# Queueing the second feed-forward's weight transfers on GpSimd instead of SyncE

## The chip, the cores and the metric

The kernel runs on one core of a Trainium2 chip. Five engines work side by side, each through its own instruction queue in order: TensorE (PE, matrix products), VectorE (DVE), ScalarE (ACT), GpSimd (POOL) and SyncE (SP, which only starts transfers). A transfer (DMA) is started by an instruction in the queue of SP, POOL or ACT and is then carried out by the core's 16 DMA engines. An instruction that has to wait holds up everything behind it in its own queue. The metric is the device time of one execution in microseconds (us); lower is better.

## The reference

Three stages follow each other; batch 4, 8 heads, 768 positions, 40 features per head.

```python
# 1: recurrence over the positions, one 40x40 state per batch and head
for t in range(S):
    y[:, :, t] = einsum('bhd,bhde->bhe', rt, state)
    Sa = einsum('bhde,bhe->bhd', state, at)
    state = state * wt[:, :, None, :] - einsum('bhd,bhe->bhde', Sa, bt)
    state = state + einsum('bhd,bhe->bhde', vt, kt)
x = y.transpose(0, 2, 1, 3).reshape(3072, 320)
# 2: first feed-forward (w1, w2: 320x1024, w3: 1024x1024, w_out: 1024x320)
x = ((x @ w1) * (x @ w2)) @ w3 @ w_out
# 3: second feed-forward (w_in: 320x2048, w_out: 2048x320)
h = maximum(x @ w_in, 0.0)
out = (h * h) @ w_out
```

The feed-forward weights arrive as 64-bit floats, so they take twice the bytes of the arithmetic.

## The kernel before

The recurrence is worked in 24 chunks of 32 positions. Chunk c runs through the stages `do_x0`, `do_sa`, `do_sat`, `do_l`, `do_z` and `do_ys`, which are chained by matrix products on PE and by copies on ACT and DVE. Between the stages PE is filled with other work from a queue of items: for every two chunks the first feed-forward of 256 tokens (`a_tile`, "ab" products at line 382 and "px" products at line 440). So PE's order in this first phase is a written one, and a product that waits holds up both kinds of work. The first phase takes about the first 696 us. In the second phase, PE runs the second feed-forward alone (`b_h` and `b_o`, "ph" and "po").

Three side streams feed the first phase.

- Preparation of later chunks (`prep`, `prep_pq`, `prep_kb`), six chunks ahead. From chunk 10 on its transfers are queued on POOL: the image of a chunk is loaded (`im<-img`, line 553), multiplied on POOL (lines 595 and 601), and then PE multiplies it in `prep_pq` (line 614). The results go to scratch tensors in DRAM.
- Loads and stores of each chunk on SP: `KB_d` and `Q_d` (scratch), `YR`, `YI`, `wt`, `XL`, `RX`, `vs` and `RT` for the next chunk, then the store of the chunk's output, `X_d<-yst` (line 837, two halves). After every second chunk `a_tile` loads two chunks' output back (`xf<-X_d`, `xr<-X_d`, lines 393 and 395), and PE's next "ab" product waits for it through a copy on ACT (`xh`, line 369).
- Weights. `fetch` loads a piece of a 64-bit weight into a staging buffer `raw` (line 326). ACT takes its two words apart (lines 334 and 335), DVE joins them to a 32-bit float (lines 339 and 342), and ACT and POOL split it into a high and a low part (`wuh`/`wul` at lines 966 and 967, `wih`/`wil` at 352 and 353, `wir` at 365 and 366).

The variable `early` is true while the weights of the first feed-forward are fetched. It is set to False at line 978, before the 36 fetches of the second feed-forward: 16 of `wo2` (320 KB each; the trace cuts digits off and names it `wo`), 4 of the last 64 rows of `win` (two transfers of 128 KB each) and 16 of `win` (256 KB each), 40 transfers in all. They share 5 `raw` buffers and 4 `wst` buffers, so fetch n+5 cannot load before line 342 of fetch n is through.

The kernel's scheduler sets the order in each queue. In the kernel before, the first five of these transfers stand on SP at chunk 3, where the memory of the first feed-forward's staging comes free (after the last `w2r` split, line 366 on POOL). The other 35 stand on SP between the loads and stores of chunks 18 to 23 and of the second phase's first input (`b_load`, line 954).

Of the kernel before, what the change touches and what calls it, by code (L numbers as in the profile page):

```python
# [245 lines left out]
def body(tc, img, rv, rd, vn, vp, raw, w1, w2, w3t, wo, win, wo2, ident, maskt, out, dbg=None):  # L246
    nc = tc.nc
    mm = nc.tensor.matmul
    act, dve, pool, sp = nc.scalar, nc.vector, nc.gpsimd, nc.sync

    with (
# [12 lines left out]
        with right, tc.manual_schedule(engines={mybir.EngineType.PE}):  # L264
# [8 lines left out]
            def staged(pl, tags, words):  # L273

                slots, n = staging.setdefault(tags, (deque(), [0]))
                if not slots:
                    t = pl.tile([128, 2048], U32, name="early", tag=tags[n[0] % len(tags)])
                    n[0] += 1
                    slots.extend(t[:, i:i + words] for i in range(0, 2049 - words, words))
                return slots.popleft()  # L280

            staging = {}
            early = True
# [14 lines left out]
            def fetch(pl, K, N, parts, dst=None, tag="fold"):  # L298

                place = None  # L300
                if early:
                    count[tag] += 1
                    if tag == "split" and count[tag] <= SPLIT_STAGED:
                        place = staged(ma, ("gh", "gl"), 1024)
                    elif tag == "fold" and not w12 and count[tag] <= FOLD_STAGED:
                        place = staged(wa, ("w1h", "w1l", "w2h"), 640)
                signed = early
                tag = "split" if early and tag == "split" else "wst"
                if dst is not None:
                    o = dst  # L310
                else:
                    o = pl.tile([128, K, N], F32, name="wst", tag=tag, bufs=bufs[tag])
                if not is64:
                    for p, f, src in parts:
                        sp.dma_start(out=o[p, f], in_=src)
                    return o
                if place is not None:
                    rt = place[:, 0:2 * K * N]
                else:
                    rt = pl.tile([128, 2 * K * N], U32, name="raw", tag="raw", bufs=bufs["raw"])  # L320
                rv_ = rt.rearrange("p (k n) -> p k n", k=K)
                at_ = MID + count["late"] // EACH
                count["late"] += not early
                with behind(mids.get(at_ - 2)):
                    for p, f, src in parts:
                        sp.dma_start(out=rv_[p, f], in_=src)
                w2_ = rt.rearrange("p (k n j) -> p k n j", k=K, j=2)
                hi, lo = w2_[:, :, :, 1], w2_[:, :, :, 0]
                top = rt.bitcast(F16).rearrange("p (k n j) -> p k n j", k=K, j=4)[:, :, :, 1]
                ou = o.bitcast(U32)  # L330


                with tc.issue_after(gate[-1]) if early and gate else behind(mids.get(min(at_, NCH - 1))), tc.issue_after(gate[-2]) if early and len(gate) > 2 else nullcontext():
                    act.activation(out=o, in_=hi.bitcast(F32), func=AF.Copy, scale=2.0 ** -112)
                    act.activation(out=lo, in_=lo, func=AF.Copy, scale=2.0 ** -29, bias=LOW)  # L335
                    if signed:
                        act.activation(out=top, in_=hi.bitcast(F32), func=AF.Copy, scale=2.0 ** -60)
                with tc.issue_after(hold[-1]) if hold else nullcontext():
                    dve.scalar_tensor_tensor(out=ou, in0=ou, scalar=3, in1=lo, op0=ALU.logical_shift_left,  # L339
                                             op1=ALU.bitwise_or)  # L340
                    if not signed:
                        dve.scalar_tensor_tensor(out=ou, in0=hi, scalar=0x80000000, in1=ou, op0=ALU.bitwise_and,
                                                 op1=ALU.bitwise_or)
                return o

            def split_w(pl, src, h, l, j, k):

                n = 512 if early else 256

                t = fetch(pl, 1, n, [(slice(0, 128), 0, wcols(src, n * j, n)[128 * k:128 * k + 128])], tag="split")  # L350
                f = slice(n * j, n * j + n)
                act.copy(out=h[:, k, f], in_=t[:, 0])
                pool.tensor_tensor(out=l[:, k, f], in0=t[:, 0], in1=h[:, k, f], op=ALU.subtract)

            def split_r(pl, two):

                n = 512 if early else 256


                t = fetch(pl, 1, n, [(slice(64 * i, 64 * i + 64), 0, wcols(src, c, n)[256:320])  # L360
                                       for i, (src, c, _) in enumerate(two)], tag="split")
                for i, (_, c, r) in enumerate(two):
                    p, q = slice(64 * i, 64 * i + 64), slice(64 - 64 * i, 128 - 64 * i)
                    f = slice(c, c + n)
                    act.copy(out=r[p, f], in_=t[p, 0])
                    pool.tensor_tensor(out=r[q, f], in0=t[p, 0], in1=r[p, f], op=ALU.subtract)
# [90 lines left out]
            def fold(solved):  # L457
# [5 lines left out]
                def load_w3(i):  # L463
                    f, g = i // 2, i % 2
                    w3[i] = fetch(wf, 4, 128, [(slice(0, 128), slice(0, 4), wcols(w3t, 128 * f, 128)[
                        512 * g:512 * g + 512, :].rearrange("(k p) f -> p k f", p=128))])
# [40 lines left out]
            with (  # L507
# [394 lines left out]
                for c in range(NCH):  # L902
                    last = c == NCH - 1
                    p = c + 6
# [73 lines left out]
            early = False  # L978
# [190 lines left out]
```

## Time and profile before

| What | Value |
|---|---|
| median of 3 runs | 1052.82 us (1050.34 to 1056.4) |
| profiled execution, its own time | 1051.49 us |
| span of the profile, first to last instruction | 1049.6 us |
| mean granted TensorE clock | 0.964 |
| PE busy | 912.6 us, 87% |
| DVE busy | 684.0 us, 65% |
| ACT busy | 476.3 us, 45% |
| POOL busy | 222.2 us, 21% |
| chain that ended last | PE 54%, DVE 19%, DMA 11%, ACT 9%, issue 4%, SP's queue 1%, POOL 1% |

All times in the rows are counted from the start of the span. The busy share of PE is an average over two different phases: in the last 350 us PE hardly pauses, while in the first phase it pauses a few us at a time, where a chunk's chain, a load or a split arrives late. A queue named SPq is SP's, POOL's own instructions appear as POOL or POOLq. In a row of the timeline the number in brackets is the time for which the engine stood still before the instruction, and what released it.

### The profile page before, as it was taken

What the parts mean: (1) busy time and instruction counts of PE and PEld (TensorE: products, weight loads), DVE (VectorE), ACT (ScalarE), POOL (GpSimd) and SP (SyncE); (2) the same over time, 40 slices, a digit from 0 to 9 for tenths busy, and PEclk for the clock granted to TensorE, in tenths of its full rate; (3) what the DMA queues carried; (4) which work ended last, traced back from release to release, by engine and by line L of the source; (5) the groups of instructions that cost most, each with busy time, mean ns of one, the idle gap of its engine ahead of it and who ended that gap; (6) DMA issues with size and microseconds to landing.
All of it is one profiled execution on the core that took longest, in us unless ns stands there. A gap on an engine that the chain in (4) does not pass through costs nothing.

```text
span 1049.6 us, 29232 instructions
## 1 busy us (share of the span) xinstructions
PE 912.6 (87%) x12240; PEld 818.8 (78%) x12240; DVE 684.0 (65%) x1366; ACT 476.3 (45%) x975; POOL 222.2 (21%) x304
## 2 busy tenths in 40 slices
PE   1346676898899899899999889999999999999996
PEld 1235454688899788789988879889899999999996
DVE  8753689569869977996798655753555554444432
ACT  2845776343353334435355546643433333434332
POOL 0242125443444343443202112310000000000000
PEclk9999688899999999989999989899999999999999
DMA  8988875665667567766665753631223121000001
GB/s 225 304 241 214 222 214 157 186 173 150 148 185 183 148 156 196 182 152 171 149 146 151 196 125 100 175 76 36 31 62 69 58 36 26 1 26 1 25 2 27
DMA packets 209389, 134.44 MB, mean 128 GB/s; under 512 B 143793, under 2 KB 184114, under 8 KB 209252
## 3 DMA queue, kind: packets, MB, share of 16 engines
q1 hardware_dynamic: 201892, 110.61, 41.3%
q0 software_dynamic: 7072, 21.57, 7.1%
q8 instruction: 98, 1.61, 0.7%
q10 hardware_dynamic: 288, 0.33, 0.1%
q14 instruction: 39, 0.32, 0.1%
HBM read 99.27 MB, written 33.19 MB: 126 GB/s over the span
## 4 chain that ended last, share of the span: by engine, by line
PE 54%; DVE 19%; DMA 11%; ACT 9%; issue 4%; SPq 1%; POOL 1%; ACTq 0%; DVEq 0%; POOLq 0%
PE ph L382 17%; PE po L1029 16%; PE ab L382 9%; PE px L440 4%; DMA im<-img 4%; DVE T L678 2%; DVE tmp L675 2%; DVE yst L834 2%; DMA raw<-w3t 2%; DVE RX L830 2%; PE pat L822 2%; PE pat L793 1%; ACT raw L335 1%; DVE wst L339 1%; DMA early<-w 1%
## 5 line engine op out<-in xcount | busy, mean ns | idle before, releaser
L1029 PE MATMUL po<-wul,rh 128*128 128x320 f32 x384 | 118.1, 308 | 0.0
L1029 PE MATMUL po<-wuh,rh 128*128 128x320 f32 x384 | 118.0, 308 | 0.0
L1029 PE MATMUL po<-wuh,rl 128*128 128x320 f32 x384 | 117.3, 307 | 0.0
L382 PE MATMUL ph<-xh,wih 128*128 128x512 f32 x192 | 75.7, 394 | 0.7 <-issue 0.7
L382 PE MATMUL ph<-xh,wil 128*128 128x512 f32 x192 | 75.3, 392 | 0.0
L382 PE MATMUL ph<-xl,wih 128*128 128x512 f32 x192 | 74.9, 390 | 0.0
L1029 PEld LDWEIGHTS po<-wul,rh 128*128 128x128 f32 x384 | 72.0, 188 | 3.6
L1029 PEld LDWEIGHTS po<-wuh,rh 128*128 128x128 f32 x384 | 72.0, 188 | 3.5
L419 ACT CAST gh<-g 128x256 fp32r<-128x256 f32 x96 | 38.9, 405 | 75.8 <-DVE g L414 69.5
L1029 PEld LDWEIGHTS po<-wuh,rl 128*128 128x128 f32 x384 | 71.8, 188 | 0.0
L440 PE MATMUL px<-wph,gh 128*128 128x320 f32 x192 | 66.5, 346 | 5.5 <-DVE x L445 4.6
L678 DVE TENSOR_TENSOR T<-T,tmp 128x31 f32<-128x31 f32 (+20 forms) x170 | 66.4, 391 | 3.5
L675 DVE TENSOR_TENSOR tmp<-PT,T 128x31 f32<-128x31 f32 (+20 forms) x170 | 64.2, 378 | 3.7
L420 DVE TENSOR_TENSOR gl<-g,gh 128x256 fp32r<-128x256 f32 x96 | 47.5, 497 | 26.6 <-ACT gh L419 26.1
L413 ACT COPY a_sb<-ab 128x256 f32<-128x256 f32 x96 | 35.6, 371 | 63.4 <-PE ab L382 62.9
L382 PE MATMUL ab<-xh,w1h 128*128 128x256 f32 x192 | 58.9, 307 | 6.0 <-ACT xh L369 5.9
L822 PE MATMUL pat<-YI,YR 128*40 128x72 f32 (+1 forms) x1536 | 56.6, 234 | 6.0 <-DVE qt L621 4.0
L440 PE MATMUL px<-wph,gl 128*128 128x320 f32 x192 | 61.1, 318 | 0.5 <-DVE gl L420 0.5
L822 PEld LDWEIGHTS pat<-YI,YR 128*40 128x40 f32 x1536 | 51.9, 123 | 11.3 <-DVE qt L621 4.5
L440 PE MATMUL px<-wpl,gh 128*128 128x320 f32 x192 | 60.5, 315 | 0.0
L382 PE MATMUL ph<-xq,wir 128*128 128x512 f32 x192 | 59.2, 390 | 0.0
L382 PE MATMUL ab<-xl,w1h 128*128 128x256 f32 x192 | 58.4, 304 | 0.7 <-DVE xl L370 0.6
(539 smaller groups left out, 2450.6 us busy)
## 6 DMA issues: line engine op xcount, KB each, us to landing
raw<-w3t SPq DMA_DIRECT2D x16, 512.0 KB
YR<-KB_d SPq DMA_DIRECT2D x48, 160.0 KB
im<-img POOLq DMA_DIRECT2D x28, 240.0 KB, 4.7
wt<-AW_d SPq DMA_DIRECT2D x24, 214.5 KB
raw<-wo SPq DMA_DIRECT2D x16, 320.0 KB
RX<-vp SPq DMA_DIRECT2D x24, 208.0 KB
vs<-rv SPq DMA_DIRECT2D x24, 208.0 KB
KB_d<-kn POOLq DMA_DIRECT2D x14, 320.0 KB, 5.9
```

The costliest lines, as they stand in the source:

```text
L335: act.activation(out=lo, in_=lo, func=AF.Copy, scale=2.0 ** -29, bias=LOW)
L382: mm(out=ps, lhsT=seq[i][0], rhs=seq[i][1], start=(i == 0), stop=(i == 7))
L413: act.copy(out=a_sb, in_=ps[:, 0])
L419: act.copy(out=t["gh"][:, ff], in_=g)
L420: dve.tensor_tensor(out=t["gl"][:, ff], in0=g, in1=t["gh"][:, ff], op=ALU.subtract)
L440: mm(out=ps, lhsT=a_, rhs=b_, start=(k == 0 and i == 0), stop=(k == 7 and i == 2))
L675: dve.tensor_tensor(out=tv, in0=Pv[:, :, s, s + 1:n].unsqueeze(3).to_broadcast(sh), in1=Tv[:, :, s, 0:s + 1].unsqueeze(2).to_broadcast(sh) ...
L678: return dve.tensor_tensor(out=o, in0=o, in1=tv, op=ALU.subtract).ins
L822: mm(out=ps[64 * y:64 * y + D, b, 72 * z:72 * z + n], lhsT=YR[:, u], rhs=YI[:, u, 0:n], start=True, stop=True, tile_position=(0, 64 * y))
L830: dve.tensor_tensor(out=o, in0=v[r, :, :, C:72], in1=decay.unsqueeze(3).to_broadcast([D, 2, HZ, D]), op=ALU.mult)
L834: dve.tensor_tensor(out=yst[r, :, 2 * g:2 * g + 2].rearrange("p z b t -> p b z t"), in0=v[r, :, :, 0:C], in1=wt[c][r, 2 * g:2 * g + 2, :, ...
L1029: mm(out=po[j][g], lhsT=a_, rhs=b_, start=(ff == 0 and i == 0), stop=(ff == 15 and i == 2))
```

## The change

In `fetch`, the transfer of a late fetch is started by POOL instead of SP. Early fetches stay on SP.

```diff
                 with behind(mids.get(at_ - 2)):
                     for p, f, src in parts:
-                        sp.dma_start(out=rv_[p, f], in_=src)
+                        (sp if early else pool).dma_start(out=rv_[p, f], in_=src)
```

All 40 transfers move. PE's order stays the same; the scheduler shifts a few neighbours on SP, ACT and DVE. POOL's queue at chunk 3, where the first five transfers come to stand; `w1r` and `w2r` are the last splits of the first feed-forward's weights, `im<-img` is the image of chunk 10. Before:

```order
45 L366 TENSOR_TENSOR w1r<-wst,w1r 64x512
46 L366 TENSOR_TENSOR w2r<-wst,w2r 64x512
47 L665 MEMSET T 128x32
48 L623 TENSOR_TENSOR qt<-qt,msk 128x256
49 L553 DMA im<-img 40x1536 x2
50 L595 TENSOR_TENSOR im<-im,wi 104x512
```

And now:

```order
45 L366 TENSOR_TENSOR w1r<-wst,w1r 64x512
46 L366 TENSOR_TENSOR w2r<-wst,w2r 64x512
47 L665 MEMSET T 128x32
48 L326 DMA raw<-wo 128x640 x5
49 L623 TENSOR_TENSOR qt<-qt,msk 128x256
50 L553 DMA im<-img 40x1536 x2
51 L595 TENSOR_TENSOR im<-im,wi 104x512
```

The five transfers stand ahead of `qt` and of the image's load. SP's queue at chunk 21, the loads for chunk 22 and the stores and reloads of the output of chunks 20 and 21. Before:

```order
404 L326 DMA raw<-win 64x512
405 L738 DMA YR<-KB_d 64x2x320
406 L735 DMA YI<-rd 40x32x32
407 L736 DMA YI<-vn 32x32x40
408 L738 DMA YR<-KB_d 64x2x320
409 L326 DMA raw<-win 64x512
410 L837 DMA X_d<-yst 40x4x128
411 L742 DMA wt<-AW_d 104x528
412 L727 DMA XL<-AW_d 40x512 x2
413 L730 DMA XL<-Q_d 32x4x128 x2
414 L732 DMA RX<-vp 32x1664
415 L837 DMA X_d<-yst 40x4x128
```

And now:

```order
393 L738 DMA YR<-KB_d 64x2x320
394 L735 DMA YI<-rd 40x32x32
395 L736 DMA YI<-vn 32x32x40
396 L738 DMA YR<-KB_d 64x2x320
397 L837 DMA X_d<-yst 40x4x128
398 L742 DMA wt<-AW_d 104x528
399 L727 DMA XL<-AW_d 40x512 x2
400 L730 DMA XL<-Q_d 32x4x128 x2
401 L732 DMA RX<-vp 32x1664
402 L837 DMA X_d<-yst 40x4x128
```

The two weight transfers are gone; the rest keeps its order. The last part is POOL's queue at the end of the first phase, where before the 16 `wil` splits stood in one piece without any transfer. Now:

```order
214 L326 DMA raw<-win 128x512
215 L366 TENSOR_TENSOR wir<-wst,wir 64x256 x2
216 L326 DMA raw<-win 128x512 x4
217 L353 TENSOR_TENSOR wil<-wst,wih 128x256 x4
218 L326 DMA raw<-win 128x512
219 L353 TENSOR_TENSOR wil<-wst,wih 128x256
220 L326 DMA raw<-win 128x512 x2
221 L353 TENSOR_TENSOR wil<-wst,wih 128x256 x2
```

The transfers now alternate with the splits and no longer stand behind SP's loads of the second phase's input.

## Rows read from the trace of the kernel before

**Rows 1.** The page: busy time, share and instructions of an engine, and one VectorE group.
```profile
PE 912.6 (87%) x12240; PEld 818.8 (78%) x12240; DVE 684.0 (65%) x1366; ACT 476.3 (45%) x975; POOL 222.2 (21%) x304
...
L420 DVE TENSOR_TENSOR gl<-g,gh 128x256 fp32r<-128x256 f32 x96 | 47.5, 497 | 26.6 <-ACT gh L419 26.1
```

**Rows 2.** PE's timeline at chunk 3: start, us, what, idle before and releaser.
```profile
204.66 0.44 PE L614 MATMUL pat<-im 40*32 40x64 f32 x8 [4.18 <-POOL im L601]
205.95 1.11 PE L614 MATMUL pat<-im 40*32 40x64 f32 x56 [0.85 <-POOL im L601]
```

**Rows 3.** The chain that ended last, at the same place: start, us, what.
```profile
192.51 0.74 POOL qt L623
193.25 0.49 POOL im L553
193.74 7.99 DMA im<-img
...
201.87 1.46 POOL im L595
```

**Rows 4.** SP's timeline at chunk 3.
```profile
185.09 2.32 SPq L749 DMA_DIRECT2D RT<-rv  x2
192.37 2.25 SPq L326 DMA_DIRECT2D raw<-wo  x5
...
197.60 6.19 SPq L736 DMA_DIRECT2D YI<-vn  x1
```

**Rows 5.** Two stretches at chunk 3: busy times, clock, DMA share, GB/s.
```profile
194.00:202.00 8.00, 6.48 (x156) 5.99 (x150) 5.77 (x14) 2.30 (x6) 0.38 (x2) 1.00 0.95 297
204.00:210.00 6.00, 4.49 (x87) 3.86 (x91) 3.30 (x5) 0.37 (x1) 3.14 (x6) 0.50 0.83 202
```

**Rows 6.** Transfers issued by POOL: ns of one issue (min/median/max); us to landing for L553.
```profile
L553 POOL DMA_DIRECT2D im<-img x28: 505/520/556, 193.2 to 495.2; - x28
...
DMA to landing us min/median/max: 3.6/4.7/8.0
```

**Rows 7.** The same for the lines L638 of POOL and SP.
```profile
L638 POOL DMA_DIRECT2D KB_d<-kn x14: 549/558/561, 216.3 to 515.7; - x14
...
L638 SPq DMA_DIRECT2D KB_d<-kn x10: 327/355/948, 26.9 to 195.2; - x10
```

**Rows 8.** PE's timeline late in the first phase: three of its pauses.
```profile
623.55 0.58 PE L382 MATMUL ab<-xh,w1h 128*128 128x256 f32 x1 [4.81 <-ACT xh L369]
...
664.19 0.58 PE L382 MATMUL ab<-xh,w1h 128*128 128x256 f32 x1 [1.09 <-ACT xh L369]
665.37 0.58 PE L382 MATMUL ab<-xl,w1h 128*128 128x256 f32 x1 [0.59 <-DVE xl L370]
```

**Rows 9.** SP's timeline at chunks 19 to 23.
```profile
569.72 0.33 SPq L742 DMA_DIRECT2D wt<-AW_d  x1
...
611.24 0.60 SPq L326 DMA_DIRECT2D raw<-win  x1
611.95 0.46 SPq L837 DMA_DIRECT2D X_d<-yst  x1
612.52 1.52 SPq L742 DMA_DIRECT2D wt<-AW_d  x1
...
616.21 0.36 SPq L837 DMA_DIRECT2D X_d<-yst  x1
...
620.11 0.40 SPq L393 DMA_DIRECT2D xf<-X_d  x1
...
669.07 2.33 SPq L326 DMA_DIRECT2D raw<-win  x5
...
675.89 3.60 SPq L326 DMA_DIRECT2D raw<-win  x4
```

**Rows 10.** Two stretches after PE's pauses: busy times, clock, DMA share, GB/s.
```profile
624.00:628.00 4.00, 3.86 (x41) 3.38 (x40) 0.56 (x2) 0.08 (x1) 0.00 (x0) 0.50 0.42 134
664.00:668.00 4.00, 3.21 (x13) 2.92 (x14) 3.28 (x7) 1.96 (x6) 2.07 (x4) 0.50 0.81 149
```

## The prediction

> **What bounds the kernel now.** I read the page first. PE is busy 87% of the span [rows 1], POOL 21%, so POOL has room, and SP computes nothing. A gain or loss can come only where PE stands still in the first phase and a transfer is behind it. I therefore went through PE's pauses in the timeline, and for each followed the chain of waits and SP's timeline back to the transfer. Two places touch the moved transfers.
>
> At chunk 3, PE stands still for 4.18 + 0.85 = 5.03 us ahead of the product on the image of chunk 10 [rows 2]. The chain shows why: POOL starts the load of the image at 193.25, it lands at 193.74 + 7.99 = 201.73, POOL multiplies, PE goes on [rows 3]. The median landing of this load is 4.7 us, this one is the slowest of 28 with 8.0 [rows 6]. The reason stands on SP: at 192.37 it starts the first five transfers of `wo2` [rows 4], five times 128 x 640 words of 4 bytes, 1.64 MB. From 194 to 202 the DMA engines are busy for 0.95 of the time and move 297 GB/s [rows 5]. Behind the five, SP itself is held: one `YI` transfer takes 6.19 us to issue [rows 4]. After PE's pause the clock is at 0.50, which is the 1.2 GHz level, over the whole stretch from 204 to 210 [rows 5].
>
> At chunk 21, PE stands still for 4.81 us until the reloaded output of chunks 20 and 21 is copied [rows 8]. SP's timeline shows the path: a weight transfer at 611.24, the first half's store at 611.95, `wt` at 612.52 with 1.52 us (at chunk 19 the same line took 0.33), the second half's store at 616.21, the reload at 620.11 [rows 9].
>
> **The change part by part.** It removes 40 issues from SP and puts 40 on POOL, nothing is added to what is moved.
>
> Issue time. On SP an issue of the like shape (128 x 640) has a median of 355 ns, on POOL 558 [rows 7]. On SP 40 x 0.355 = 14 us go, on POOL 40 x 0.558 = 22 us come. POOL is busy for 21% of the span [rows 1], and after the last preparation (chunk 17) only the splits stand in its queue, so 35 of the 40 cost nothing directly. A POOL issue that waits for a free `raw` buffer holds only the splits behind it. They in turn hold `wst` buffers; PE does not wait for them before the second phase. Cover gone, it would be some 0.6 us of PE's order, one issue.
>
> The first five are the exception. They stand ahead of `qt` and of the image's load. They wait for the same thing as on SP (the last `w2r` split, which POOL itself runs), so they start at about 192.4 as before. Then 5 x 0.558 = 2.8 us pass before `qt`. This path is the one on which PE waits, and in PE's pause nothing else has work that could cover it: the whole delay of the landing counts.
>
> How late does the image land? The transfer has 2 x 40 rows of 1536 words, 0.49 MB. Before, it was alone in POOL's queue while the 1.64 MB went through SP's. Now both are in POOL's queue, 2.13 MB, the image last, and SP's own small transfers run beside them without being held. No row shows this queue under such a load, so bounds. From below: if only the total rate counts, 2.13 MB at 297 GB/s take 7.2 us, from 194 to 201.2, no later than now: 0. From above: if POOL's queue gets half of the 297 from the start, 2.13 / 148.5 gives 14.3 us, landing at 208.3: +6.6. Between them stand two values: the 8.0 us of now from an issue 2.8 us later gives +2.8; full rate until 197.6, when SP issues `YI` [rows 4], then half, gives 1.07 MB by then, the other 1.06 MB in 7.1 us, landing at 204.7: +3.0. I take +3.0. The pause of 5.03 us becomes some 8. The clock falls to 0.50 after it already now [rows 5], so I count nothing more for it.
>
> The Trainium skill bears on this place (DMA: Bandwidth & Descriptors, "Queues, rings and completion order"): each DMA engine goes round between the queues that have work, a packet at a time. If that were an equal share of bytes, the image would before have landed after twice its 0.49 MB, at about 194 + 3.3 = 197.3; the row has 201.73, so an equal share of bytes is not borne out here. For the kernel after, the rule speaks against the change: within one queue the image comes after the 1.64 MB, and by an equal share the sum would have +6.6 here instead of +3.0.
>
> What SP gains at the same place: it is no longer held from 187.41 (185.09 + 2.32) to 192.37, nor in the 6.19 us issue [rows 4]. What it issues there is for chunk 4 and later, and the chain there runs through POOL's image and not through SP [rows 3]: 0, and nothing below, since none of it has to wait for more than now.
>
> Chunk 21. The weight transfer at 611.24 goes: 0.60 us and the gap behind it, 611.95 - 611.24 = 0.7 us, off SP's path to the second store. If the 1.52 us of `wt` was caused by it too, 1.52 - 0.33 = 1.2 us more. The same bytes now come from POOL in these microseconds and share the DMA engines, which can slow the store and the reload; one reload pause of 4.81 us bounds the gain, and a store that lands a microsecond later the loss. Range -1.9 to +1, I take -1.0.
>
> End of the first phase. Before, SP issued five transfers together at 669.07 and four from 675.89, behind the second phase's first input [rows 9]. On POOL they can start as buffers come free, so decoding comes forward by some us. PE's pauses there are 1.09 + 0.59 us [rows 8], and what ends them is the copy of the reloaded output on ACT and DVE. DVE now takes `xl` ahead of two other instructions, ACT puts more decoding ahead of the third copy. From -1.7 to +0.6; I take -0.3.
>
> Sum: 3.0 - 1.0 - 0.3 = +1.7 us on the profiled execution's 1051.49 us, 1053.2. The median of the runs is 1052.82, 1.33 above the profiled one, so the forecast is 1054.5 us. The measurement tells a change of about 0.5% (5.3 us: under 1047.6 or over 1058.1) from none.
>
> **The rivals.**
> - Half rate for POOL's queue (slower). Place: the image of chunk 10. SP's small transfers take half of the DMA engines throughout, so the image lands 6.6 us later. 6.6 - 0.7 = +5.9: 1052.82 + 5.9 = 1058.7. It decides from a landing after about 207.7, 15 us after the first of the five starts (6.0 us later than now, less the 0.7 of chunk 21). For it: the engines are at 0.95 already, and without the 6.19 us hold SP sends more at this time. Against it: SP's stream begins only with its loads for chunk 4, when part of the 1.64 MB has gone.
> - No later landing. The bytes are the same and the image was last before too, so it lands at 201.7 again: 0 - 1.0 = 1051.8. For it: 0.95 busy. Against it: 2.8 us later issue and the new competition.
> - Late pauses shrink so far that the clock holds (faster). If `wt` is short again (-1.9), and PE's pauses at chunks 21 and 23 become short enough that the clock stays at its full level, the 4 us at 0.50 in each of the two stretches [rows 10] are done in half the time, -2 each: -5.9 with no delay at chunk 3, 1046.9. For it: both pauses end in a reload. Against it: the store and reload take most of the 4.81 us and are not moved, and the clock falls at 664 after pauses of 1.09 and 0.59.
> - GpSimd's issues are held by DVE (slower). Rows: the 28 issues of the image load took 505 to 556 ns, through a phase in which DVE is busy 65% [rows 1, 6], so nothing of the kind shows. If each of the five waited for one DVE instruction of 0.497 us [rows 1], 2.5 us would come on top: +4.2, 1057.0; with longer holds over 1058.1, and I count it as slower. The Trainium skill has such a rule (SBUF — State Buffer, "SBUF: two separate sides"): transfers issued from GpSimd need descriptors that GpSimd writes, and a DVE instruction that takes both ports locks it out; the trace does not agree so far.
>
> **How the numbers follow.** Forecast 0.48, landing no later 0.16, half rate 0.22, held issues 0.04, faster 0.10. The first two are within 0.5%: 0.64. Slower by over 0.5%: 0.26. Faster: 0.10. The range goes from the edge of the faster case, 1048, to 1061, a little above the half-rate case, since a longer pause could also lengthen the stretch at the low clock. The forecast's own range is 1051 to 1057.
>
> **What would show it.** Right: the five issues stand on POOL from about 192.4 with 0.56 us each, `YI` on SP no longer takes 6 us, the image lands at about 204.7 and PE's pause ahead of line 614 is about 8 us; `wt` at chunk 21 is short or the second store comes a microsecond earlier; the ACT-released pause there is about 4 us. Wrong: the image lands at 202 or earlier, or after 207; a new pause of PE on a split of POOL; or the clock held after a late pause.

## The result: slower by 1.1%, outside the range that was forecast

The changed kernel takes 1064.7 us (median of 5, 1058.5 to 1071.6), the kernel before 1053.0 in the same comparison (1050.3 to 1056.4): ratio 1.011, 95% interval 1.007 to 1.015, so 8 to 16 us more. The forecast was 1054.5 with a range of 1048 to 1061. The profiled execution after took 1064.3 us, span 1062.5.

PE's instructions stand in the same order in both kernels, so the two traces can be laid beside each other by the first matmul of each chunk's L761. The table gives how much later than in the trace of before it starts (us); "second phase" is the first matmul of `ph`. The last three lines are from experiments below, and the line "before, again" is the kernel before profiled once more.

| start of chunk | 4 | 5 | 20 | 21 | 22 | 23 | second phase |
|---|---|---|---|---|---|---|---|
| after | +1.6 | +5.3 | +7.2 | +10.0 | +10.1 | +11.1 | +12.9 |
| before, again | +6.9 | +6.8 | +6.7 | +6.0 | +6.0 | +4.5 | +3.7 |
| rest of `wo2` on GpSimd | +1.2 | +1.5 | +6.2 | +7.1 | +7.0 | +6.4 | +6.9 |
| `win` on GpSimd | +1.6 | +2.5 | +2.2 | +1.6 | +1.6 | +5.1 | +9.0 |
| five later (SyncE) | +1.5 | -1.3 | -0.6 | -0.2 | -0.2 | -0.7 | -0.8 |

Read steps, not heights: two traces of the very same instructions differ by up to 6.9 us in the first four chunks. After gains its delay in three places: 3.7 us in chunk 4, 2.8 us in chunk 20, and 2.8 us from chunk 22 to the second phase; the rest (1.6 before chunk 4, 1.9 spread over 5 to 19) is no more than the two traces of before differ by.

**Where the image of chunk 10 is waited for.** POOL's timeline after, answering to [rows 3, 4]:

```profile
194.19 2.71 POOL L326 DMA_DIRECT2D raw<-wo  x5 [0.20 <-POOL T L665]
196.97 0.72 POOL L623 TENSOR_TENSOR qt<-qt,msk 128x256 f32<-128x256 f32 x1
197.64 1.06 POOL L553 DMA_DIRECT2D im<-img  x2
207.29 1.17 POOL L595 TENSOR_TENSOR im<-im,wi 104x512 f32<-104x512 f32 x1 [8.59 <-DMA im<-img]
```

PE's timeline there, answering to [rows 2], SP's, answering to [rows 4], and one stretch (columns as in [rows 5]):

```profile
209.80 0.44 PE L614 MATMUL pat<-im 40*32 40x64 f32 x8 [7.77 <-POOL im L601]
211.08 1.12 PE L614 MATMUL pat<-im 40*32 40x64 f32 x56 [0.84 <-POOL im L601]
```
```profile
198.61 6.06 SPq L736 DMA_DIRECT2D YI<-vn  x1
```
```profile
198.00:202.00 4.00, 4.00 (x90) 3.64 (x88) 3.27 (x8) 1.11 (x3) 0.70 (x2) 1.00 1.03 398
```

The five stand on POOL with 2.71 / 5 = 0.54 us each. POOL multiplies 207.29 - 194.19 = 13.1 us after the first of them; before it was 201.87 - 192.37 = 9.5 us [rows 3, 4]: 3.6 later. PE's pause is 8.61 us instead of 5.03. In the 4 us from 198 the DMA engines are full and move 398 GB/s; over the 8 us from 195.8 to 203.8, a stretch as long as that of before, it is 308 GB/s, hardly more than the 297 of before [rows 5]. After the pause PE runs at 0.50, from 208 to 214, as it did before. SP's `YI` issue still takes 6 us.

**The late chunks.** In order of time, on four engines of the changed kernel: the weight transfers on POOL (some of them, and two splits among them), SP's reload of each of the last three pairs of chunks and, for the first two pairs, the second store ahead of it, ACT's copy of the reloaded tile, and PE's pauses.

```profile
577.86 1.09 POOL L326 DMA_DIRECT2D raw<-wo  x2 [2.89 <-DVE wst L342]
578.97 1.72 POOL L967 TENSOR_TENSOR wul<-wst,wuh 128x320 fp32r<-128x320 f32 x2
580.63 0.55 POOL L326 DMA_DIRECT2D raw<-wo  x1
...
620.39 1.05 POOL L326 DMA_DIRECT2D raw<-win  x2 [13.66 <-ACT a_sb L413]
...
623.84 2.08 POOL L326 DMA_DIRECT2D raw<-win  x4 [1.51 <-DVE wst L342]
...
671.58 1.07 POOL L326 DMA_DIRECT2D raw<-win  x2 [0.28 <-DVE wst L342]
```
```profile
576.97 0.36 SPq L837 DMA_DIRECT2D X_d<-yst  x1
...
580.69 0.40 SPq L393 DMA_DIRECT2D xf<-X_d  x1
...
624.99 0.36 SPq L837 DMA_DIRECT2D X_d<-yst  x1
631.84 0.39 SPq L393 DMA_DIRECT2D xf<-X_d  x1
...
672.11 0.39 SPq L393 DMA_DIRECT2D xf<-X_d  x1
```
```profile
585.73 0.62 ACT L369 CAST xh<-xf 128x512 fp32r<-128x512 f32 x1 [1.08 <-DMA xf<-X_d]
...
634.88 0.62 ACT L369 CAST xh<-xf 128x512 fp32r<-128x512 f32 x1 [6.26 <-DMA xf<-X_d]
...
677.75 0.62 ACT L369 CAST xh<-xf 128x512 fp32r<-128x512 f32 x1 [3.98 <-DMA xf<-X_d]
```
```profile
582.81 0.64 PE L778 MATMUL pat<-idt,SA 128*104 128x128 f32 x4 [1.53 <-ACT SA L773]
587.46 1.15 PE L793 MATMUL pat<-RT,vs 104*64 104x64 f32 x32 [1.81 <-ACT vs L780]
...
635.54 0.58 PE L382 MATMUL ab<-xh,w1h 128*128 128x256 f32 x1 [6.85 <-ACT xh L369]
...
673.82 0.41 PE L440 MATMUL px<-wph,gh 128*128 128x320 f32 x1 [0.85 <-ACT gh L419]
678.42 0.58 PE L382 MATMUL ab<-xh,w1h 128*128 128x256 f32 x1 [3.55 <-ACT xh L369]
```

Rows of before that the prediction did not need, on SP, on ACT and on PE (its second store of chunk 19 starts at 570.09):

```profile
574.10 0.40 SPq L393 DMA_DIRECT2D xf<-X_d  x1
...
576.88 1.31 SPq L326 DMA_DIRECT2D raw<-wo  x3
...
660.39 0.39 SPq L393 DMA_DIRECT2D xf<-X_d  x1
```
```profile
577.12 0.62 ACT L369 CAST xh<-xf 128x512 fp32r<-128x512 f32 x1 [0.72 <-DMA xf<-X_d]
...
663.52 0.62 ACT L369 CAST xh<-xf 128x512 fp32r<-128x512 f32 x1 [0.42 <-DMA xf<-X_d]
```
```profile
578.90 1.15 PE L793 MATMUL pat<-RT,vs 104*64 104x64 f32 x32 [1.47 <-ACT vs L780]
```

One instruction of DVE in chunk 20, in after and then in before:

```profile
578.62 2.85 DVE L420 TENSOR_TENSOR gl<-g,gh 128x256 fp32r<-128x256 f32 x1
```
```profile
572.12 1.10 DVE L420 TENSOR_TENSOR gl<-g,gh 128x256 fp32r<-128x256 f32 x1
```

Two intervals are to be read here: from the start of the last store to that of the reload (the reload waits until the store has landed), and from the reload to the copy that waits for it.

- Chunks 18+19: the reload takes 585.73 - 580.69 = 5.0 us, before 577.12 - 574.10 = 3.0. In before, SP's queue has the three weight transfers at 576.88, behind the reload; in after POOL issues three from 577.86, into the store and the reload. ACT works in order, so its `xh` copy holds `vs`, on which PE waits 1.81 us (before 1.47, in its second trace 0.72).
- Chunk 20 has a second new pause, 1.53 us for `SA`, and it is not the reload's. DVE's `gl` at 578.62 takes 2.85 us instead of 1.10: it ends at 581.47, 0.3 us after the end of POOL's issue of 580.63, ahead of which POOL ran two `wul` splits. In before the splits at this place follow each other with no issue between them, and DVE gets its turn after the first. ACT's `gh` waits for what stands behind `gl` on DVE, and `SA` stands behind `gh` on ACT.
- Chunks 20+21: the store takes 631.84 - 624.99 = 6.9 us, before 620.11 - 616.21 = 3.9 [rows 9], beside seven weight transfers that POOL issued from 620.39 to 627.55 (in before SP issued two there, at 616.68). PE's pause is 6.85 instead of 4.81 us [rows 8] (3.53 in the second trace of before).
- Chunks 22+23: the reload takes 5.6 us, before 3.1. PE waits 3.55 + 0.85 us, where before it waited 1.09 + 0.59 [rows 8] and 0.76 us ahead of them: 2.0 more.

The DMA engines are full in two of these stretches, and after the pauses of chunk 20 the clock falls for some 3 us at a place where in before it stood at full speed:

```profile
580.00:585.00 5.00, 3.47 (x26) 3.21 (x25) 2.78 (x4) 2.56 (x6) 2.16 (x3) 1.00 1.00 313
588.00:592.00 4.00, 4.00 (x41) 3.71 (x38) 2.19 (x4) 0.00 (x0) 0.00 (x0) 0.58 0.45 79
624.00:628.00 4.00, 4.00 (x34) 3.79 (x27) 3.53 (x6) 3.93 (x11) 4.00 (x7) 1.00 1.00 239
```

### The profile page after: what moved, and what is told of

Its sections match the earlier page's. It is cut to its first block, busy times and chain, and to the rows that moved or that the text cites. A ratio compares the mean times of both kernels' runs of the same rounds, so it can differ in the third digit from the quotient of the medians.

```text
span 1062.5 us, 29229 instructions
## 1 busy us (share of the span) xinstructions
PE 914.5 (86%) x12240; PEld 820.5 (77%) x12240; DVE 688.4 (65%) x1366; ACT 476.0 (45%) x975; POOL 241.2 (23%) x344
## 3 DMA queue, kind: packets, MB, share of 16 engines
q0 software_dynamic: 10016, 32.06, 10.2%
## 4 chain that ended last, share of the span: by engine, by line
PE 55%; DVE 18%; DMA 13%; issue 5%; ACT 4%; SPq 3%; POOL 1%; DVEq 0%; ACTq 0%; POOLq 0%
PE ph L382 17%; PE po L1029 16%; PE ab L382 9%; PE px L440 5%; DMA im<-img 4%; DVE tmp L675 3%; DMA raw<-w3t 2%; DVE T L678 2%; DVE yst L834 2%; DVE RX L830 2%; DMA X_d<-yst 2%; PE pat L822 2%; PE pat L793 1%; DMA xf<-X_d 1%; SPq L749 1%
## 5 line engine op out<-in xcount | busy, mean ns | idle before, releaser
L675 DVE TENSOR_TENSOR tmp<-PT,T 128x31 f32<-128x31 f32 (+20 forms) x170 | 66.5, 391 | 3.7
L822 PEld LDWEIGHTS pat<-YI,YR 128*40 128x40 f32 x1536 | 51.4, 122 | 10.1 <-ACT YR L809 3.1
```

The lines of the kernel that those rows point to most:

```text
L675: dve.tensor_tensor(out=tv, in0=Pv[:, :, s, s + 1:n].unsqueeze(3).to_broadcast(sh), in1=Tv[:, :, s, 0:s + 1].unsqueeze(2).to_broadcast(sh) ...
L822: mm(out=ps[64 * y:64 * y + D, b, 72 * z:72 * z + n], lhsT=YR[:, u], rhs=YI[:, u, 0:n], start=True, stop=True, tile_position=(0, 64 * y))
```

## The experiments

The theory: on SP the weight transfers stood in one order with the stores and reloads that PE waits for, mostly behind them. In a queue of their own they start without waiting for those, and share the 16 DMA engines with them. The rivals: the cost of 40 issues on GpSimd; the new order of ACT's and DVE's instructions, which the scheduler chose; a drift between runs. In all diffs `count["late"]` is the number of the transfer's fetch, 1 to 36 (1 to 16 are `wo2`). Where an expectation numbers transfers (10 to 16, 17 to 25, 26 to 35), it counts the fetches from 0: in the diffs these are 11 to 17, 18 to 26 and 27 to 36.

A part of the second rival falls by the traces of before and after alone: DVE's order is the same in both up to 662 us of before, and ACT's too but for a few copies at 212 to 215 us. The new orders can therefore act at the image and behind the reload of chunks 22+23, but not in chunks 18 to 21.

**Only the first five on GpSimd**, in two comparisons.

```
-    (sp if early else pool).dma_start(out=rv_[p, f], in_=src)
+    (pool if 1 <= count["late"] <= 5 else sp).dma_start(out=rv_[p, f], in_=src)
```

> Only the first five transfers of wo2 are queued on GpSimd, the other 35 stay on SyncE. Theory (the DMA engines are shared: what GpSimd queues runs beside or ahead of the critical transfers, each by its bytes): the image of chunk 10 lands about 9 us after its issue, PE's pause ahead of line 614 at chunk 3 is about 8.6 us instead of 5.0, and nothing else changes: before + 3.5 us, ratio 1.0033. Rival 1 (GpSimd's issue cost, 0.56 us each, adds up over all 40): 5/40 of the 12 us, + 1.5 us. Rival 2 (the order that the scheduler gives ACT and DVE in the last chunks): DVE's order is that of before here, so no change at the late chunks, and chunk 3 alone remains: + 0 to 3.5. Rival 3 (a drift that has nothing to do with the transfers): 0.

> Once more the kernel with only the first five transfers of wo2 on GpSimd, whose time came out 1.0 us above before (interval 0.9992 to 1.0026) while PE's pause at chunk 3 was 8.0 us instead of 4.6 to 5.0. Theory (the pause counts in full): ratio 1.003, and over both runs 1.002 or more. Rival (a part of the pause is given back at a later wait): ratio 1.001 again.

Measured: ratio 1.0009 (0.9992 to 1.0026) and 1.0012 (0.9993 to 1.0030), about +1.1 us. PE's pause is 7.18 + 0.84 us in the one trace and 7.98 + 0.85 in the other, against 5.03 and 4.56 in the two traces of before. So the pause grows by some 3.5 us as the theory says, but the time by less: the theory's sum missed here, and its rival in the second run hit. Where the rest is given back the traces do not settle, since those of before alone differ by more. This stays open.

**Only the other eleven of `wo2`**, chunks 18 to 20 (`6 <= count["late"] <= 16`), with the orders of PE, ACT and DVE exactly those of before.

> Only the other eleven transfers of wo2 (about chunks 18 to 20) are queued on GpSimd. The orders of PE, ACT and DVE are exactly those of before. Theory: the store and the reload of the outputs of chunks 18 and 19 run beside these transfers, the reload takes some 5 us instead of 3, PE pauses about 1.5 us twice in chunk 20 and its clock falls to 0.50 for some 3.5 us: before + 3.5 us, ratio 1.0033. Rival 1 (issue cost on GpSimd): 11/40 of 12 us, + 3.3 us, but without a longer reload. Rival 2 (shifted orders of ACT and DVE): 0, since they are not shifted. Rival 3 (drift): 0.

Measured: 1.0044 (1.0025 to 1.0064), +4.6 us. ACT and PE in chunk 20:

```profile
584.23 0.62 ACT L369 CAST xh<-xf 128x512 fp32r<-128x512 f32 x1 [1.60 <-DMA xf<-X_d]
```
```profile
580.80 0.65 PE L778 MATMUL pat<-idt,SA 128*104 128x128 f32 x4 [1.43 <-ACT SA L773]
585.97 1.15 PE L793 MATMUL pat<-RT,vs 104*64 104x64 f32 x32 [2.32 <-ACT vs L780]
```

The reload, issued at 578.95, takes 5.3 us. The same two pauses as in after, with no other order on ACT or DVE: the second rival falls for this place. The pause for `SA` comes with a `gl` of 2.85 us on DVE, as in after, and not from the reload, to which the theory put it down. The fall of the clock in chunk 20 that it expected is not there: the clock stood at 0.50 from 567.5 to 570.9, in chunk 19, and then at full speed up to 629.

**Only `win`**, chunks 20 to 23 (`count["late"] > 16`).

> Only the 24 transfers of win (chunks 20 to 23) are queued on GpSimd. Theory: the second store of chunk 21 lands after 6.8 us instead of 3.8 and PE's pause there is 6.9 instead of 4.8 us; the reload of chunk 23 takes 5.3 instead of 3.0 us and PE pauses 3.5 + 0.9 instead of 1.1 + 0.6: before + 4 us (2.1 + 2.7, less what chunk 21 gains on SP), ratio 1.004. Rival 1 (issue cost): 24/40 of 12 us, + 7 us. Rival 2 (shifted orders of ACT and DVE): + 4 as well, since DVE's order is that of the changed kernel here; the reload's landing tells it from the theory. Rival 3 (drift): 0.

Measured: 1.0079 (1.0057 to 1.0101), +8.3 us, twice the theory's figure and nearer to the first rival's 7; the lengths of the store and the reload speak for the theory, and the next run tells the two apart. SP and PE at chunks 20+21:

```profile
617.46 0.36 SPq L837 DMA_DIRECT2D X_d<-yst  x1
624.86 0.39 SPq L393 DMA_DIRECT2D xf<-X_d  x1
```
```profile
628.39 0.58 PE L382 MATMUL ab<-xh,w1h 128*128 128x256 f32 x1 [8.37 <-ACT xh L369]
```

The store takes 7.4 us and the pause is 3.6 us longer than before; at chunks 22+23 PE waits 3.89 + 0.86 us. The part is dearer alone than within after, perhaps since there chunk 20 has already delayed PE; no run shows this. The three parts sum to 1.1 + 4.6 + 8.3 = 14 us, after had 12 (8 to 16).

**All 40 on GpSimd, with a tenth of the bytes.**

```
-    (sp if early else pool).dma_start(out=rv_[p, f], in_=src)
+    (sp if early else pool).dma_start(out=rv_[p, f] if early else rv_[p, f, 0:64],
+                                      in_=src if early else src[:, 0:64])
```

> As the changed kernel, all 40 transfers on GpSimd with the same waits, but each moves only its first 64 words of 640 or 512 a row, a tenth of the bytes; the rest of the buffers is zeroed once on GpSimd, so the second feed-forward is computed with most of its weights zero. Theory (bytes on the shared DMA engines): the image of chunk 10 lands about 5 us after its issue, the reloads take 3 us, PE's pauses at chunk 3 and in chunks 20 to 23 are as short as before or shorter: 1045 to 1051 us, ratio to before 0.993 to 0.998. Rival 1 (issue cost and holds on GpSimd) and rival 2 (order of ACT and DVE): the issues and the orders are still those of the changed kernel, so 1060 to 1064, ratio 1.008 to 1.011.

Measured: 1.0001 (0.9980 to 1.0022). SP and PE at chunks 20+21:

```profile
618.50 0.36 SPq L848 DMA_DIRECT2D X_d<-yst  x1
621.75 0.39 SPq L404 DMA_DIRECT2D xf<-X_d  x1
```
```profile
578.71 0.65 PE L789 MATMUL pat<-idt,SA 128*104 128x128 f32 x4 [1.52 <-ACT SA L784]
...
625.34 0.58 PE L393 MATMUL ab<-xh,w1h 128*128 128x256 f32 x1 [3.29 <-ACT xh L380]
```

The issues are all there (0.55 us each), and the 12 us are gone: what lengthened the store, the reloads and the landing of the image is the bytes. The store takes 3.25 us, the pause for the image is 2.42 + 0.96, the pauses at chunks 22+23 are 0.51 + 0.52. So the first rival falls as an account of the 12 us.

It does not fall whole. In chunk 20 DVE's `gl` takes 2.85 us here too, and PE pauses 1.52 us for `SA` as in after. Both are in the four traces in which these transfers are issued among the `wul` splits (after, this one, the eleven of `wo2` alone and the run with the image first below; 1.43 to 1.53 us), and the pause is in no other. A pause of 1.1 us in chunk 19 grows to 1.7 in all six kernels that issue `wo2` among the splits there, beside a `tmp` of DVE (L675 in after) that takes 1.83 instead of 0.90 us. So some 2 us come from where the issues stand in GpSimd's queue, and no bytes are needed for them. They are one reason why the kernel is no faster than before, though its other pauses are shorter, which the theory had not said; its trace was also 5.4 us late already at chunk 4.

**The same bytes, later.** GpSimd reads one element of the reloaded tile ahead of the weights, so that they wait in its queue until the reload has landed.

```
+    if n > 8:                                   # in the reload of chunks 2n and 2n + 1
+        seen = ma.tile([1, 1], F32, name="seen", tag="seen")
+        keep["g", n] = pool.tensor_copy(out=seen, in_=t["xf"][0:1, 0, 0:1])
...
-    with behind(mids.get(at_ - 2)):
+    with behind(keep["g", 9 + (count["late"] > 17) + (count["late"] > 26)].ins if count["late"] > 10 else None):
```

> As the changed kernel, but three one-element copies on GpSimd, each of which reads the reloaded outputs of chunks 18+19, 20+21 and 22+23, stand in its queue ahead of the weight transfers 10 to 16, 17 to 25 and 26 to 35: these are issued only when the reload of their chunk has landed. Theory (the loss in the late chunks is the store and the reload sharing the DMA engines with the weights): the second store of chunk 21 takes 3.3 to 3.9 us to the reload's issue instead of 6.9, the reloads of chunks 19 and 23 take 3 us instead of 5 and 5.6, PE's pauses are 3.3 to 4.8 at chunk 21 and under 1.5 at chunk 23: the changed kernel less 7, 1057, ratio to before 1.002 to 1.005; more if weights that come later make decoding late at the start of the second phase. Rival 1 (issue cost on GpSimd): as the changed kernel, 1063 to 1065, ratio 1.009 to 1.011, for the issues are all there and three copies more.

Measured: 1.0014 (0.9990 to 1.0038), 10 us under after by the two ratios, and a little faster than the theory's range.

```profile
628.58 0.17 POOL L398 COPY seen<-xf 1x1 f32<-1x1 f32 x1 [5.52 <-DMA xf<-X_d]
631.98 3.66 POOL L326 DMA_DIRECT2D raw<-win  x7 [3.23 <-issue]
```
```profile
621.48 0.36 SPq L840 DMA_DIRECT2D X_d<-yst  x1
625.50 0.39 SPq L393 DMA_DIRECT2D xf<-X_d  x1
```

The store takes 4.0 us and PE's pause is 4.12. Queue, number of issues and bytes are those of after; when they run has changed, and with it where the issues of chunk 20 stand: `gl` takes 1.10 us again and the pause for `SA` is gone. The orders of DVE and ACT are those of after up to the reload of chunks 22+23. In this trace the pause for the image is 6.25 us, though nothing was changed there, so the two traces are not to be subtracted place by place.

All traces of this document together settle the stores and reloads. In the three that issue all bytes of `win` on GpSimd without waiting for a reload (after, `win` alone, the image first), the store of chunk 21 takes 6.2 to 7.4 us, PE's pause behind it 6.4 to 8.4 and the reload of chunk 23 4.5 to 6.0. In the eleven others these are 3.0 to 4.6, 3.2 to 5.5 and 2.8 to 3.6 us. What the new orders of DVE and ACT behind the last reload cost by themselves was not tested.

**The first five behind the image, in GpSimd's queue** (issue order only: the fetches 1 to 5 behind the image load's instruction).

> As the changed kernel, but in GpSimd's queue the first five transfers of wo2 stand behind the load of the image of chunk 10 instead of ahead of it. Theory (what is ahead in a queue goes first, and what runs beside shares): the image is alone ahead of the five, SyncE's small transfers run beside, it lands 4 to 5 us after its issue, PE's pause ahead of line 614 is 2.5 + 0.9 us as in the run with a tenth of the bytes (changed kernel 7.8 + 0.8), the changed kernel less 5: about 1059, ratio to before 1.005. Rival (an equal share of bytes between the transfers in flight, whatever their order): landing 8 to 9 us after the issue as in the changed kernel, 1063, ratio 1.009 to 1.011.

Measured: 1.0067 (1.0043 to 1.0091), 4.6 us under after by the two ratios, though their intervals overlap; it lies between theory and rival.

```profile
195.14 1.05 POOL L553 DMA_DIRECT2D im<-img  x2
196.21 2.71 POOL L326 DMA_DIRECT2D raw<-wo  x5
201.67 1.18 POOL L595 TENSOR_TENSOR im<-im,wi 104x512 f32<-104x512 f32 x1 [2.75 <-DMA im<-img]
```

POOL multiplies 6.5 us after the load's start (9.7 in after), PE pauses 1.93 + 1.15 us. Within one queue the order counts: this the rival does not allow. On SP the `YI` issue here takes 7.75 us.

**The kernel before, with the first five later on SyncE**: behind chunk 4's first store (231 us instead of 192), and behind chunk 12's (419 us).

```
-    with behind(mids.get(at_ - 2)):
+    with behind(keep["st", 4].ins if 1 <= count["late"] <= 5 else None):    # second kernel: keep["st", 12]
```

> The kernel before, all 40 transfers on SyncE, but the first five of wo2 are queued behind the first store of chunk 4's outputs (about 25 us later). Theory: the image of chunk 10 lands 4 to 5 us after its issue instead of 8, PE's pause at chunk 3 falls from 4.2 + 0.9 to 2.4 + 0.9 us: before less 1.6 to 3, ratio 0.997 to 0.9985. SyncE's 6 us issue of a YI transfer at chunk 3 is short if the five's bytes cause it, and stays if they do not. Rival (the five were hidden anyway, or the image of chunk 11 is hit instead): ratio 1.000 or above.

> The kernel before with the first five transfers on SyncE behind the first store of chunk 12's outputs instead of at chunk 3; GpSimd's and ACT's orders are those of before. Theory (any place where no image is on its way does): the pause at chunk 3 is about 3 us as with the five behind chunk 4's store, and no new pause at chunks 11 to 13: ratio to before 0.995 to 0.998. Rival (the gain at chunk 4's store is run to run): 0.999 to 1.001.

Measured: 0.9961 (0.9941 to 0.9980) and 0.9982 (0.9965 to 0.9999): 4 and 2 us faster than before; the first beats the theory's range, the second lies between the theory's and the rival's. PE and SP of the first:

```profile
203.86 0.32 PE L614 MATMUL pat<-im 40*32 40x64 f32 x8 [1.92 <-POOL im L601]
205.15 0.79 PE L614 MATMUL pat<-im 40*32 40x64 f32 x56 [0.97 <-POOL im L601]
```
```profile
198.52 2.27 SPq L736 DMA_DIRECT2D YI<-vn  x1
```

The pause for the image is 2.89 us here and 3.02 in the second kernel. In both the scheduler also put one `gl` of DVE at chunk 3 behind a few others; what that does to the time was not tested.

**Both remedies on GpSimd, and both on SyncE** (the edits above, put together; on SyncE the later weights stand behind the last reload transfer of their chunks).

> The two remedies on GpSimd together: the first five transfers behind the load of the image of chunk 10, and the one-element copies ahead of transfers 10 to 16, 17 to 25 and 26 to 35; all 40 on GpSimd. Theory (the whole loss is what runs ahead of or beside a critical transfer, so the two remedies add): the pause at chunk 3 is about 3 us and those at chunks 21 and 23 as in the run with the copies alone; 1054.8 less 4.6, about 1050 to 1051, ratio to before 0.996 to 0.998. Rival (a queue of GpSimd's own costs something by itself, issue time or descriptors): not under before, ratio 1.000 to 1.005.

> All 40 transfers on SyncE, the first five behind the first store of chunk 4's outputs as in the run before, and those of chunks 20 and 21 (number 17 on) behind the reload of chunks 20+21, those from number 26 on behind the reload of chunks 22+23. Theory: the second store of chunk 21 takes 3.3 instead of 3.2 to 3.9 us to the reload's issue (little or nothing to gain), the reload lands in 2.8 us as before; PE's pause there is 3.3 to 4 us. The run with the first five alone less 0 to 1.5 us: 1049 to 1050.5, ratio to before 0.9945 to 0.9965. Rival (weights that come later make the decoding late): PE waits at the start of the second phase, ratio 0.997 to 1.000.

Measured: 0.9987 (0.9968 to 1.0006) and 0.9985 (0.9964 to 1.0007). With the remedies GpSimd's queue is no slower than SyncE's; neither figure can be told from before. The first lies between the theory's range and the rival's. The second lies in the rival's range, but the late decoding that the rival names is not in the trace: PE's late pauses are 3.20 and 0.84 us, and it waits 0.65 us at the start of the second phase, as before (0.66). So what the later place of `win` costs there, if anything, is open. The best ratio of all is the 0.9961 above, with the first five alone moved; the three kernels with that step on SyncE lie between 0.996 and 0.9985, so what it is worth is some 2 to 4 us.

**The kernel before, again.**

> The kernel before once more, every engine's order unchanged: how far two runs of the same instructions differ, in the time and chunk by chunk in the trace. Theory and rivals 1 and 2: ratio 1.000 within 0.002. Rival 3 (a drift between runs explains a good part of the 12 us): a ratio beyond 1.003.

Measured: 1.0007 (0.9987 to 1.0027): no drift in the time, though the trace is 3.7 us longer than the first. It had been a short one: 1051.49 against medians of 1053 to 1055. At chunk 21 it shows:

```profile
618.57 0.32 SPq L742 DMA_DIRECT2D wt<-AW_d  x1
...
621.92 0.36 SPq L837 DMA_DIRECT2D X_d<-yst  x1
```

## Why the prediction was wrong, step by step

- **The image, +3.0.** The mechanism and the place were right, the pause came out at 8.6 us where "some 8" stood. In time the five alone cost about 1.1 us (two runs), so that "the whole delay of the landing counts" is not what the time shows, and the term was, if anything, too large. The half-rate rival fell: the landing came 3.6 us later against the first issue, not 6.6. Its 1058.7 is the nearest to the time measured, but by a delay that did not come. Not counted: the low clock after the pause, 6.8 us in before, lasted 10.2 in after; in the two traces of the five alone it lasted 6.8 and 10.2.
- **"35 of the 40 cost nothing directly."** This is the step that failed. It asked what waits for POOL and for the weights, and found nothing. Which transfers are on their way when the 35 start it asked at chunk 21 alone, and it bounded the loss there by a microsecond for which no row stood. SP's order was seen as a burden on the stores and not as what kept the bulk transfers behind them. Moved alone, the eleven of `wo2` cost 4.6 us and those of `win` 8.3 us. That a waiting POOL issue "holds only the splits behind it" failed too: with the issues among the splits, DVE's `gl` took 1.75 us longer, and PE waited for it.
- **Chunk 21, -1.0.** Wrong in sign. The bound for the loss was "a microsecond later"; the store took 6.9 us instead of 3.9, in the kernel with `win` alone 7.4. Of the gain little shows: the 1.52 us of `wt` [rows 9] was an accident of that trace, since the same instruction took 0.32 in the second one, and the second store came 3.35 us behind it all the same. What holds that store is SP's own loads for the next chunk: DVE has written the last of `yst` by 618.5 in that trace, but `wt`, `XL` and `RX` stand between the two stores, and their issues follow each other without a gap up to 621.9. In the kernel with `win` alone the two stores start 4.2 us apart, in before 4.3.
- **End of the phase, -0.3.** Wrong in sign: "decoding comes forward" means bytes come forward, onto the reload, which took 5.6 us instead of 3.1. PE's waits grew by 2.0 us.
- **Chunk 20** was in no term and no rival, though the SP rows of before had it: the weights at 576.88 behind the reload at 574.10. After gained 2.8 us of its delay there, by the longer reload and by the hold of DVE; how much by each is open, since the two overlap.
- **SP's 6.19 us issue** was put down to the five standing in SP's queue. It stays at 6.06 when they stand in POOL's and is 7.75 when they run just beside it. With the five at this place it took 3.9 to 7.9 us over all traces (3.93 in the second one of before), and 2.3 to 2.9 in the four in which they are away or a tenth: it goes with the bytes in flight, whichever queue they are in.
- **The other rivals.** No issue was held on GpSimd (0.52 to 0.59 us for the 40); it was DVE that was held. The clock fell after the pauses for chunks 20+21 and 22+23 as it did before.

The rule that each DMA engine goes round between the queues with work (the Trainium skill, DMA: Bandwidth & Descriptors, "Queues, rings and completion order") was weighed for the image alone. The trace agrees with it at the stores of chunk 21: the run with a tenth of the bytes has the same transfers in SP's queue, and there the second store took 3.25 us, against 6.9 with GpSimd's full transfers in the other queue; by which rule the engines shared their time it does not show. The Trainium skill (DMA: Bandwidth & Descriptors, "Issuing engines are not separate DMA queues") says that what several engines issue runs on the same 16 DMA engines. The trace agrees, by the same 3.25 and 6.9 us.

## What to carry to other kernels

Before transfers move to another queue, list for each what critical transfer it stood behind in the old one: that order was a priority, and a queue of its own gives it up. If the move is wanted, make the bulk wait for the landing that it must not disturb (a one-element copy on the issuing engine did, for 10 us here). For the first five a later place in the same queue was the cheaper cure: 2 to 4 us faster than before. And look at what else the new queue carries: issues put among GpSimd's splits moved the splits, and an instruction of another engine waited for them.

## What was not expected of the hardware

The same issue on SP (the `YI` transfer of L736 at one place of the program) took from 2.3 to 7.9 us, longer with the large transfers in flight beside it, also when GpSimd had issued them. An instruction of DVE took 2.85 us instead of 1.10 while GpSimd ran two splits and an issue, whether the transfers were full or a tenth. And a repeated trace of the same instructions differs by up to 7 us within the first 200 us and by 3.7 us at the end; the clock stood at 0.50 at other places in those 200 us, for 41 us against 31, and since half the clock loses half of that time, this accounts for at most 5 of the 7 us.
